# Q's memory slots by a selection product, its other columns by crossbar DMA, and scores on four column groups straight from the key ring

## The chip, the cores and the metric

The kernel runs on one core of one Trainium2 chip. The metric is the device time of one execution, in microseconds (us). "Before" and "after" are always the two kernels. Quoted times are medians. Ratios are computed from the mean time of one kernel's fast runs over the mean of the other's fast runs of the same rounds, so they are not quite the ratios of the medians.

## The reference, cut to what matters

```python
# x: (1, 2048, 640) bf16; 32 heads of 128; M = 8 memory slots; segments of 32 tokens
mem = mem0
for s in range(64):
    h = concat([mem, layernorm(x)[segment s]])           # 8 + 32 rows
    q, k, v = h @ Wq, h @ Wk, h @ Wv                     # 32 heads
    p = softmax(where(mask, q @ k.T * Dh**-0.5, -1e9))   # 40 x 40 for each head
    o = (p @ v) @ Wo
    mem = o[:8]                                          # the next segment needs this
    outs.append(o[8:])
h = x + concat(outs)
out = h + ((relu(g) * u) @ W_down)                       # g, u: gate and up products of layernorm(h)
```

Only the 8 memory rows tie one segment to the next. This makes a serial loop of 64 rounds; the feed-forward part at the end is one large block of matrix products.

## The kernel before

In each segment (a round of the loop) TensorE (PE) projects 32 columns: the 8 memory slots, and up to 24 "riders", tokens of later segments that fill the tile. Keys and queries of tokens are parked in a ring (`Kr`, `Qr`) until their segment comes. A projection leaves its result token by token; scores need it with the head dimension on the partitions, so it has to be transposed.

K goes through the crossbar (the DMA's transposing path, `DMA_TRANSPOSE` in the traces) into `KS`; Q goes through TensorE (`trans8`):

```python
project(a, ks, 1, (0, 1), BQ, spare=40)              # K of 32 columns
to_tok(BQ[0], 0, "act"); to_tok(BQ[1], 1, "dve")
dma_t(KS[...], tokp[0][:, :], ...)                   # crossbar, on the SP queue
loads()
...
project(a, ks, 0, (0, 1), (P0, P1), spare=40)        # Q
if s == NSEG - 2:
    load_gate_up()                                   # weights of the feed-forward part
...
project(a, ks, 2, (0, 1), (P2, P3), (0, 1), spare=16)    # a first piece of V
trans8(tok[2], ("tok", 2), tok[3], ("tok", 3), T0)       # eight 128x128 transposes
copy_op("dve", Qr[:, :, q, 0:M], slots(T0, 0, M), ...)   # Qm: the memory slots of Q
kx_mem(KS[:, :, 0:M], ("KS",))                           # KX: memory slots of K; waits for KS
if nr:
    evac_q(T0, t0, nr, M, "act")                         # riders of Q into the ring
    evac_k(KS, ("KS",), t0, nr, M, "dve")                # riders of K into the ring
# ... cut: a store and a load of the normalization rows ...
project(a, ks, 2, (0, 1), (P2, P3), (2, 3, 4), spare=24) # the rest of V
# ... cut ...
scores(s)                                                # reads KX and Qr
```

The program issues each engine's instructions in the order in which they are written, and in the traces below they run in that order. So the place of a copy in this list is its place in the queue of VectorE (DVE). In the same way all transfers that are written without another engine go to one queue, SP's, in order.

The scores are products with 64-column and 40-column tiles of `KX`, a copy that puts memory slots and tokens of two heads side by side:

```python
for k in range(8):
    for e in range(2):
        for cg in range(2):
            h = 4 * k + 2 * cg + e
            n = 64 - (SEG - M) * e
            i = pe.matmul(bank(...)[64 * cg:64 * cg + n, ...], KX[:, h, 0:n], Qr[:, h, q, :], ...)
```

Finally, the kernel fixes where the output product (the "Wo pass") falls within lines of 256 instructions of PE's stream. It does this with four marks, one for each s%4, and fills up with repeated weight loads in the projections (`spare`):

```python
PE_FIRST, PE_LINE = 64, 256
MARKS = (130, 108, 130, 130)
...
wo_pass(T1, MARKS[s % 4] if s > 3 else None)
...
G.align(PE_FIRST, PE_LINE)
```

The softmax here doesn't subtract the row's maximum and nothing guards it: scores larger than these inputs give would overflow.

## Time and profile before

| | before |
|---|---|
| Time, median of 3 runs (range) | 1146.69 us (1143.68 to 1147.58) |
| Span of the profiled execution | 1142.5 us |
| PE busy | 1083.2 us, 95% |
| PE idle just before the scores | 8.7 us |
| Period of a segment, mean over segments 4 to 60 | 14.00 us |
| First score, after the start of that segment's K projection | 7.42 us |
| DVE's first copy out of `KS`, on the same clock | 6.91 us |

X stands for the start of a segment's K projection throughout.

These lines are from the page of the kernel before: its span, the busy time of each engine, and the chain of work that ended last.

```profile
span 1142.5 us, 55213 instructions
...
PE 1083.2 (95%) x26294; PEld 573.2 (50%) x24948; DVE 614.2 (54%) x1603; ACT 357.4 (31%) x729; POOL 279.7 (24%) x567
...
PE 84%; DMA 7%; DVE 4%; SPq 3%; issue 1%; ACT 0%; DVEq 0%
PE ps L409 30%; PE ps L387 14%; PE ps L621 14%; PE ps L987 10%; DMA KS<-tok 4%; PE ps L429 3%; PE ps L549 3%; PE ps L635 3%; PE ps L1020 3%; SPq L355 3%; DMA Wo<-in_A_Wo_dram 3%; PE ps L586 2%; DVE TBf L525 1%; DVE act_r L526 1%; PE ps L659 1%
```

Read: TensorE is the limit nearly everywhere. The transfer of `KS` makes up 4% of the chain.

The second view is one line of the groups of the kernel before: line, engine, operation, names, shapes, count, then busy time and mean ns of one, then idle time before it and who ended it.

```profile
L549 PE MATMUL ps<-Qr,KX 128*64 128x40 bf16 (+1 forms) x2048 | 40.7, 184 | 8.7 <-DVE KX L438 8.5
```

In the 64 segments PE waits 8.7 us in all for what the scores need. One wait, in the last segment, is 4.5 us of that.

The third view is the timeline of segment 33 of the kernel before (X = 510.99): start, duration, instruction, and in brackets the idle time before it with its releaser. First DVE, then PE.

```profile
515.53 0.69 DVE L438 CAST tok<-ps 128x512 bf16<-128x512 f32 x1 [1.47 <-PE ps L387]
516.94 0.29 DVE L438 COPY Qr<-ps 128x256 bf16<-128x256 bf16 x1 [0.72 <-PE ps L429]
517.79 0.23 DVE L438 COPY KX<-KS 128x256 bf16<-128x256 bf16 x1 [0.56 <-DMA KS<-tok]
517.93 0.42 DVE L438 COPY Kr<-KS 128x256 bf16<-128x256 bf16 x2
```

```profile
516.28 0.62 PE L429 MATMUL ps<-ident,tok 128*128 128x128 bf16 x8
516.85 1.48 PE L409 MATMUL ps<-W,act_r 128*32 128x512 bf16 x24
518.26 0.63 PE L549 MATMUL ps<-Qr,KX 128*64 128x40 bf16 x32
```

The Qm copy fills a gap in which DVE would wait for `KS` anyway. The copy out of `KS` that the scores need (`KX`) is the first thing after the landing. The rider copies (`Kr`) come behind it. PE goes from V straight into the scores.

### The profile page before, as it was taken

What the parts mean: (1) busy time and instruction counts of PE and PEld (TensorE: products, weight loads), DVE (VectorE), ACT (ScalarE), POOL (GpSimd) and SP (SyncE); (2) the same over time, 40 slices, a digit from 0 to 9 for tenths busy, and PEclk for the clock granted to TensorE, in tenths of its full rate; (3) what the DMA queues carried; (4) which work ended last, traced back from release to release, by engine and by line L of the source; (5) the groups of instructions that cost most, each with busy time, mean ns of one, the idle gap of its engine ahead of it and who ended that gap; (6) DMA issues with size and microseconds to landing.
All of it is one profiled execution on the core that took longest, in us unless ns stands there. A gap on an engine that the chain in (4) does not pass through costs nothing.

```text
span 1142.5 us, 55213 instructions
## 1 busy us (share of the span) xinstructions
PE 1083.2 (95%) x26294; PEld 573.2 (50%) x24948; DVE 614.2 (54%) x1603; ACT 357.4 (31%) x729; POOL 279.7 (24%) x567
## 2 busy tenths in 40 slices
PE   5589999999999999999999999999999978999998
PEld 2345555555555555555455555555555545443443
DVE  3245656565656565656565666565656542553522
ACT  2113333333333333333333333333333312221220
POOL 1013333333323242414141414141414130000000
PEclk9989999999999999999999999999999998999999
DMA  9934454445444454545655455444545395132100
GB/s 354 377 75 78 65 72 65 72 66 75 65 75 66 72 73 65 78 92 80 87 74 92 78 93 72 73 74 63 74 60 71 58 229 166 35 81 71 29 18 24
DMA packets 214103, 102.45 MB, mean 90 GB/s; under 512 B 188032, under 2 KB 203456, under 8 KB 213872
## 3 DMA queue, kind: packets, MB, share of 16 engines
q1 hardware_dynamic: 196016, 82.96, 38.4%
q0 software_dynamic: 17664, 15.94, 7.3%
q8 instruction: 201, 3.29, 1.3%
q14 instruction: 30, 0.25, 0.1%
q10 hardware_dynamic: 192, 0.01, 0.0%
HBM read 36.79 MB, written 7.21 MB: 39 GB/s over the span
## 4 chain that ended last, share of the span: by engine, by line
PE 84%; DMA 7%; DVE 4%; SPq 3%; issue 1%; ACT 0%; DVEq 0%
PE ps L409 30%; PE ps L387 14%; PE ps L621 14%; PE ps L987 10%; DMA KS<-tok 4%; PE ps L429 3%; PE ps L549 3%; PE ps L635 3%; PE ps L1020 3%; SPq L355 3%; DMA Wo<-in_A_Wo_dram 3%; PE ps L586 2%; DVE TBf L525 1%; DVE act_r L526 1%; PE ps L659 1%
## 5 line engine op out<-in xcount | busy, mean ns | idle before, releaser
L409 PE MATMUL ps<-W,act_r 128*32 128x512 bf16 x6209 | 436.6, 383 | 15.5 <-DVE act_r L526 4.3
L355 POOL DMA_DIRECT2D Vr<-Vp x376 | 188.2, 508 | 564.8 <-ACT Vp L436 381.2
L409 PEld LDWEIGHTS ps<-W,act_r 128*32 128x32 bf16 x6209 | 168.7, 97 | 199.8 <-issue 104.6
L436 ACT ACTIVATE tok<-ps 128x512 bf16<-128x512 f32 x191 | 110.6, 595 | 268.6 <-PE ps L387 209.6
L621 PE MATMUL ps<-Wo,oT 128*32 128x160 bf16 x8320 | 161.1, 237 | 10.9 <-DMA Wo<-in_A_Wo_dram 8.8
L387 PE MATMUL ps<-W,act_r 128*32 128x512 bf16 x1671 | 168.2, 379 | 0.0
L621 PEld LDWEIGHTS ps<-Wo,oT 128*32 128x32 bf16 x8320 | 147.2, 99 | 40.6 <-DVE oT L438 29.3
L438 DVE CAST tok<-ps 128x512 bf16<-128x512 f32 x131 | 90.6, 692 | 128.5 <-PE ps L387 68.2
L436 ACT ACTIVATE Qr<-ps 128x768 bf16<-128x768 bf16 (+3 forms) x110 | 69.2, 658 | 86.7 <-DVE Qr L438 79.4
L409 PE MATMUL ps<-W,act_e 128*32 128x512 bf16 x900 | 89.2, 381 | 0.0
L387 PE MATMUL ps<-W,act_e 128*32 128x512 bf16 x900 | 88.8, 379 | 0.0
L674 DVE TENSOR_TENSOR ox<-ps,rx 128x512 bf16<-128x512 f32 x128 | 82.5, 686 | 2.2
L355 POOL DMA_DIRECT2D attn_d<-wtok x64 | 46.9, 732 | 113.6 <-ACT wtok L436 113.6
L525 DVE STREAM_TRANSPOSE TBf<-ps 128x160 f32<-128x160 f32 x64 | 22.4, 351 | 94.5 <-PE ps L621 94.5
L1002 DVE TENSOR_TENSOR hT<-g,ps 128x512 bf16<-128x512 bf16 (+1 forms) x56 | 38.4, 688 | 54.5 <-PE ps L987 50.3
L406 PEld LDWEIGHTS <-act_r 128*32 128x32 bf16 x1433 | 42.8, 96 | 48.9 <-issue 13.5
L987 PE MATMUL ps<-xn2T,Wg 128*128 128x512 bf16 x260 | 65.2, 382 | 0.0
L987 PE MATMUL ps<-xn2T,Wu 128*128 128x512 bf16 x260 | 64.6, 379 | 0.0
L1020 PE MATMUL ps<-Wd,hT 128*128 128x320 bf16 (+1 forms) x240 | 63.3, 300 | 0.0
L1000 ACT ACTIVATE g<-ps 128x512 bf16<-128x512 f32 (+1 forms) x56 | 32.4, 593 | 93.8 <-PE ps L987 93.8
L387 PE MATMUL ps<-Wd,hT 128*128 128x320 bf16 x208 | 56.9, 299 | 0.0
L429 PE MATMUL ps<-ident,tok 128*128 128x128 bf16 x664 | 50.9, 220 | 5.2 <-DVE tok L438 3.3
(92 smaller groups left out, 1127.4 us busy)
## 6 DMA issues: line engine op xcount, KB each, us to landing
Vr<-Vp POOLq DMA_DIRECT2D x124, 48.8 KB, 1.9
W<-in_A_Wk_dram SPq DMA_DIRECT2D x2, 2560.0 KB, 12.9
W<-in_A_Wq_dram SPq DMA_DIRECT2D x2, 2560.0 KB, 25.2
W<-in_A_Wv_dram SPq DMA_DIRECT2D x2, 2560.0 KB, 27.2
Wo<-in_A_Wo_dram SPq DMA_DIRECT2D x2, 2560.0 KB, 28.5
xt<-in_A_x_dram SPq DMA_DIRECT2D x30, 160.0 KB, 3.0
Vr<-Vp POOLq DMA_DIRECT2D x128, 32.5 KB, 2.3
attn_d<-wtok POOLq DMA_DIRECT2D x64, 40.0 KB, 3.8
```

What stands on the lines that cost most here:

```text
L355: add(eng, lambda e: e.dma_start(dst, src), r=r, w=w, dma=True)
L387: return pe.add_instruction(mybir.InstMatmult(name=nc.get_next_instruction_name(), engine=mybir.EngineType.PE, ins=[pe.lower_ap(rhs), pe.l ...
L406: pe.ldweights(act[:, c, :], tile_position=(0, 32 * g))
L409: ins = pe.matmul(*a, start=(c == 0), stop=(c == DC - 1), skip_group_check=True)
L429: ins = pe.matmul(bank_bf(b)[:, k * 128:(k + 1) * 128], t[:, (k % 4) * 128:(k % 4 + 1) * 128], ident[:, :], is_transpose=True)
L436: add("act", lambda a: a.activation(dst, src, ACTF.Copy), r=r, w=w)
L438: add("dve", lambda v: v.tensor_copy(dst, src), r=r, w=w)
L621: i = pe.matmul(bank(bk)[32 * gg:32 * gg + 32, 0:160], oT[:, hb, :], w[:, gg], start=(hb == ORDER[0]), stop=(hb == ORDER[31]), skip_group_ ...
L674: add("dve", lambda v, kh=kh: v.tensor_tensor(ox[:, :, kh, :], src[:, :, kh, 0:128], ap(rx, kh, [[2, 4], [0, 128]]), ALU.mult), r=[B(b0 + ...
L987: ins = pe.matmul(bank(bk), w[:, c, lo:lo + 128], xn2T[par][:, c, :], start=(c == 0), stop=(c == DC - 1))
L1002: add("dve", lambda v: v.tensor_tensor(hT[par][lo:128, j, :], g1[gi][lo:128, :], bank(bu)[lo:128, :], ALU.mult), r=[B(bu), ("g1", gi)], w= ...
L1020: i = pe.matmul(*a, start=(j == 0), stop=(j == FC - 1), skip_group_check=True)
```

## The change

The intent is to take work off TensorE and VectorE:

1. Only the 8 memory slots of Q are needed at once. TensorE gets them with a selection product: eight products with 32 moving columns of the identity in place of eight 128-column transposes (`pick_mem`). The riders of Q go through the crossbar into `QS`, as K does.
2. The extra query tokens of every fourth segment (`fin`) go through the crossbar too.
3. The scores run on four column groups of 32, with memory slots straight from `KS` and tokens straight from the ring `Kr`. `KX` and its two copies in each segment go.
4. Orders move: `evac_k` comes ahead of the Qm copy, since the scores now need the ring; loads wait for `KS`; the normalization of later rows moves behind the attention; half of the transposes of `om` become full-width; marks are chosen anew.

The core of the diff, with cuts marked by "...":

```diff
-    MARKS = (130, 108, 130, 130)
+    MARKS = (150, 98, 114, 130)
...
+    def pick_mem(bk):
+        def f(pe):
+            for k in range(8):
+                ins = pe.matmul(bank(bk)[:, 32 * k:32 * k + 32], tok[2 + k // 4][:, (k % 4) * 128:(k % 4 + 1) * 128],
+                                ap(ident, 0, [[32, 4], [1, M]]), start=True, stop=True, skip_group_check=True)
+            return ins
...
+    def trans_q():
+        dma_t(QS[:].rearrange(...), tokp[1][:, :], [("tok", 2), ("tok", 3)], [("QS",)])
...
             for k in range(8):
-                for e in range(2):
-                    for cg in range(2):
-                        h = 4 * k + 2 * cg + e
-                        n = 64 - (SEG - M) * e
-                        i = pe.matmul(bank((P0, P1)[e])[64 * cg:64 * cg + n, 40 * k:40 * k + 40], KX[:, h, 0:n],
+                for a in range(2):
+                    for g in range(4):
+                        h = 4 * k + g
+                        p, lh = (32 * (g ^ 1), Kr[q][:, h, :]) if a == 0 else (32 * g, KS[:, h, 0:M])
+                        i = pe.matmul(bank((P0, P1)[g % 2])[p:p + (M if a else 32), 40 * k:40 * k + 40], lh,
                                       Qr[:, h, q, :], start=True, stop=True, skip_group_check=True)
...
         def fin():
-            trans8(tok[2], ("tok", 2), tok[3], ("tok", 3), T0)
-            evac_q(T0, t0, 32, 0, "act")
+            trans_q()
+            late.append(lambda: evac_q(QS, ("QS",), t0, 32, 0, "act"))
...
-                dma(xt[:, :], x_ap[128 * e2:128 * e2 + 128, :], w=[("xt",)])
+                dma(xt[:, :], x_ap[128 * e2:128 * e2 + 128, :], r=[("KS",)], w=[("xt",)])
...
                 to_tok(P0, 2, "act")
                 to_tok(P1, 3, "dve")
+                if nr:
+                    trans_q()
...
             if not last:
-                trans8(tok[2], ("tok", 2), tok[3], ("tok", 3), T0)
-                copy_op("dve", Qr[:, :, q, 0:M], slots(T0, 0, M), [B(T0)], [("Qm", q)])
-            kx_mem(KS[:, :, 0:M], ("KS",))
+                pick_mem(T0)
             if nr:
-                evac_q(T0, t0, nr, M, "act")
                 evac_k(KS, ("KS",), t0, nr, M, "dve")
+            if not last:
+                copy_op("dve", Qr[:, :, q, 0:M], bank(T0)[:, 0:256].rearrange("p (h t) -> p h t", t=M), [B(T0)], [("Qm", q)])
...
+                evac_q(QS, ("QS",), t0, nr, M, "act")        # behind exp_x
...
-        trans_om()
+        trans_om(128 if s % 4 < 2 else 32)
...
-        kx_x(seg_slot(s + 1))
```

More of the change, by code (lines that the diff above doesn't have):

```diff
@@ L271, in build_kernel @@
     tok = [tokp[i // 2][:, 512 * (i % 2):512 * (i % 2) + 512] for i in range(4)]
-    KX = ar.alloc("KX", [128, H, 2 * SEG], BF16)
     KS = ar.alloc("KS", [128, H, SEG], BF16)
     Kr = [ar.alloc(f"Kr{i}", [128, H, SEG], BF16) for i in range(RING // SEG)]
+    QS = ar.alloc("QS", [128, H, SEG], BF16)
     Qr = ar.alloc("Qr", [128, H, RING // SEG, M + SEG], BF16)
@@ L337, in build_kernel @@
         add("dve", lambda v, g=g: v.memset(mbd[32 * g:32 * g + M, 1, 8 * g:8 * g + 8], BIG), r=[("mbd",)], w=[("mbd",)])
-    add("dve", lambda v: v.memset(KX[:], 0.0), w=[("KX", "m"), ("KX", "x")])
+    for b in (P0, P1):
+        add("dve", lambda v, b=b: v.memset(bank(b), 0.0), w=[B(b)])
     add("dve", lambda v: v.memset(oT[:], 0.0), w=[("oT", "m"), ("oT", "x")])
@@ L432, in trans8 @@
         add("pe", f, r=[k0, k1, ("ident",)], w=[B(b)])
+    def pick_mem(bk):
[4 more added lines that the diff above has]
+            return ins
+        add("pe", f, r=[("tok", 2), ("tok", 3), ("ident",)], w=[B(bk)])
+    def trans_q():
+        dma_t(QS[:].rearrange("p h t -> p (h t)").rearrange("p (k r) -> p k r", r=128), tokp[1][:, :],
+              [("tok", 2), ("tok", 3)], [("QS",)])
     def copy_op(eng, dst, src, r, w):
@@ L455, in evac_k, with evac_q @@
             copy_op(eng, Kr[q][:, :, o:o + m], src[:, :, lo:lo + m], [skey], [("Kr", q)])
-    def evac_q(b, t0, n, lo, eng):
+    def evac_q(src, skey, t0, n, lo, eng):
         for q, o, m, lo in pieces(t0, n, lo):
-            copy_op(eng, Qr[:, :, q, M + o:M + o + m], slots(b, lo, lo + m), [B(b)], [("Qr", q)])
+            copy_op(eng, Qr[:, :, q, M + o:M + o + m], src[:, :, lo:lo + m], [skey], [("Qr", q)])
     def seg_slot(s):
@@ L529, in build_kernel @@
     oTe_keys = [("oTe", q) for q in range(4)]
-    def kx_mem(src, skey):
-        copy_op("dve", ap(KX, 0, [[4 * SEG, 16], [3 * SEG, 2], [1, M]]), src.rearrange("p (k e) t -> p k e t", e=2), [skey],
-                [("KX", "m")])
-    def kx_x(q):
-        copy_op("dve", ap(KX, SEG, [[4 * SEG, 16], [1, 2 * SEG]]), ap(Kr[q], 0, [[2 * SEG, 16], [1, 2 * SEG]]), [("Kr", q)],
-                [("KX", "x")])
     def scores(s):
@@ L544, in f @@
             for k in range(8):
-                for e in range(2):
-                    for cg in range(2):
-                        h = 4 * k + 2 * cg + e
-                        n = 64 - (SEG - M) * e
-                        i = pe.matmul(bank((P0, P1)[e])[64 * cg:64 * cg + n, 40 * k:40 * k + 40], KX[:, h, 0:n],
+                for a in range(2):
[3 more added lines that the diff above has]
+                        i = pe.matmul(bank((P0, P1)[g % 2])[p:p + (M if a else 32), 40 * k:40 * k + 40], lh,
                                       Qr[:, h, q, :], start=True, stop=True, skip_group_check=True)
             return i
-        add("pe", f, r=[("KX", "m"), ("KX", "x"), ("Qm", q), ("Qr", q)], w=[B(P0), B(P1)])
+        add("pe", f, r=[("KS",), ("Kr", q), ("Qm", q), ("Qr", q)], w=[B(P0), B(P1)])
     def s_view(lo, hi):
@@ L595, in norm_om, with trans_om @@
             r=[B(T1), ("rm",)], w=[("om",)])
-    def trans_om():
+    def trans_om(tile):
         def f(pe):
             for a in range(2):
-                for c in range(4):
-                    i = pe.matmul(bank_bf(T1)[32 * c:32 * c + 32, a * 128:(a + 1) * 128], om[:, a, 32 * c:32 * c + 32],
+                for c in range(0, 128, tile):
+                    i = pe.matmul(bank_bf(T1)[c:c + tile, a * 128:(a + 1) * 128], om[:, a, c:c + tile],
                                   ident[:, :], is_transpose=True)
@@ L761, in opening_back @@
             else:
-                evac_q(bk, 32 * (n - 1), 32, 0, eng)
+                evac_q(slots(bk, 0, SEG), B(bk), 32 * (n - 1), 32, 0, eng)
             return
@@ L765, in opening_back @@
         if j == 1:
-            kx_mem(slots(bk, 0, M), B(bk))
+            copy_op("dve", KS[:, :, 0:M], slots(bk, 0, M), [B(bk)], [("KS",)])
             evac_k(slots(bk, 0, SEG), B(bk), 64, RID, M, "act")
@@ L769, in opening_back @@
             copy_op("dve", Qr[:, :, q, 0:M], slots(bk, 0, M), [B(bk)], [("Qm", q)])
-            evac_q(bk, 64, RID, M, "act")
+            evac_q(slots(bk, 0, SEG), B(bk), 64, RID, M, "act")
     for j in (1, 0):
@@ L785, in build_kernel @@
         opening_back(j, 2, P2)
-    kx_x(seg_slot(0))
     scores(0)
@@ L874, in loads @@
                 ln1_load(nb, xt, ("xt",))
+            if s % 4 == 1 and s - 2 in EARLY:
+                e = EARLY.index(s - 2)
+                dma(xn2_d[:, :, 128 * e:128 * e + 128], chunks_of(at[:, :]), r=[("at",)], w=[("xn2_d", e)])
+                if ln:
+                    ln1_load(nb, xt, ("xt",))
         if s == 0:
@@ L884, in build_kernel @@
                   [("tok", 0), ("tok", 1)], [("KS",)])
-            loads()
             for f in late:
@@ L888, in build_kernel @@
             late = []
+            loads()
             if not last:
@@ L894, in build_kernel @@
                 to_tok(P1, 3, "dve")
-            n = n_rows(nb) if s % 4 == 2 and ln else 128 if e2b is not None else 0
-            if n:
-                row_scale(xt, ("xt",), n, xt, ("xt",))
-                dma_t(chunks_of(at[:, :])[:, :, 0:n], xt[0:n, :], [("xt",)], [("at",)])
+                if nr:
+                    trans_q()
             project(a, ks, 2, (0, 1), (P2, P3), (0, 1), spare=16)
             if not last:
-                trans8(tok[2], ("tok", 2), tok[3], ("tok", 3), T0)
-                copy_op("dve", Qr[:, :, q, 0:M], slots(T0, 0, M), [B(T0)], [("Qm", q)])
-            kx_mem(KS[:, :, 0:M], ("KS",))
+                pick_mem(T0)
             if nr:
-                evac_q(T0, t0, nr, M, "act")
                 evac_k(KS, ("KS",), t0, nr, M, "dve")
-            if e2b is not None:
-                dma(xn2_d[:, :, 128 * e2b:128 * e2b + 128], chunks_of(at[:, :]), r=[("at",)], w=[("xn2_d", e2b)])
-                if ln:
-                    ln1_load(nb, xt, ("xt",))
+            if not last:
+                copy_op("dve", Qr[:, :, q, 0:M], bank(T0)[:, 0:256].rearrange("p (h t) -> p h t", t=M), [B(T0)], [("Qm", q)])
             project(a, ks, 2, (0, 1), (P2, P3), (2, 3, 4), spare=24)
@@ L926, in build_kernel @@
                 v_riders(t0, nr)
-            if s % 4 == 2 and ln:
-                ln1_back(nb, chunks_of(at[:, :]), [("at",)], "pool")
+                evac_q(QS, ("QS",), t0, nr, M, "act")
         units, evac, nfin = extra_units(s)
@@ L942, in build_kernel @@
         filler(3)
-        trans_om()
+        trans_om(128 if s % 4 < 2 else 32)
         mask_x()
+        n = n_rows(nb) if s % 4 == 2 and ln else 128 if e2b is not None else 0
+        if n:
+            row_scale(xt, ("xt",), n, xt, ("xt",))
         filler(4)
@@ L957, in build_kernel @@
         pv_x(s, P0)
+        if n:
+            dma_t(chunks_of(at[:, :])[:, :, 0:n], xt[0:n, :], [("xt",)], [("at",)])
+            if s % 4 == 2:
+                late.append(lambda nb=nb: ln1_back(nb, chunks_of(at[:, :]), [("at",)], "pool"))
         if nfin:
```

## The prediction

> **What bounds it now.** The engine table has PE busy 95%; the chain that ended last is 84% PE, 7% DMA, 4% DVE. In the timeline of a plain segment (start X = 510.99 us, period 13.70) PE runs: K and Q projections, a V piece, 8 transposes of Q (X+5.29, 56 ns apart, next projection at +0.57), the rest of V, scores (X+7.27; 0.56 long), fillers, pv, Wo pass 2.40. The groups table puts 8.7 us of PE idle before scores, 5.2 before the transposes. Every fourth segment (s%4 = 3) has 8 more transposes for extra Q tokens (0.55 on the chain); such periods are 14.05. A second chain is nearly as long: K evacuated (X+3.1), crossbar transpose lands in 3.1 to 3.7 us, DVE starts the KX copy at about X+6.75, waiting for the landing 49 times of 63 (waits view). Scores start 0.28 to 1.1 us after that copy starts, mean 0.55: about 0.25 us of slack.
>
> **On PE.** (a) Pick: 32 moving columns, not 128. 56 ns apart becomes about 25: the Trainium skill ("TensorE: Matmul & The Clock Gate", the passage on the 56 ns gap) gives a floor of about 25 ns start to start; here the 40-column scores step 28 ns per round. Saves 0.2 x 62 = 13. (b) Scores in 128x32 tiles as the projections: no mode change ("TensorEngine Tiling (Array Packing)", Key Properties: that drains). Gap to the first score 309 ns against 216 between projection rounds; that and the exit, 109, shrink together by about 0.17. 16 rounds as before, of four matmuls, not two: estimated 28 to 35 ns each against 28. Saves 6 to 12. (c) Extra-Q transposes go: 15 x 0.4 = 6. (d) trans_om as two full matmuls in half the segments: two mode changes, +0.1 x 31 = +3.
>
> **Moved.** KX copies (0.42 and 0.22) leave DVE; 77 crossbar transposes (about 1.3 us of issue each) join the SP queue behind KS; I expect KS landing little changed. row_scale leaves the path before scores, the x load waits for KS: that should end single stalls (1.4 us before scores at 546.8, 0.7 at 504.5), about 3 us.
>
> **What gives gain back.** DVE's new order: wait for KS, evac_k (about 0.3), Qm copy from fp32 PSUM (about 0.42, as the 128x256 om product), then scores. Before, scores followed the landing by 0.28; now by about 0.75. PE would be ready at about X+6.95, DVE lets it go at X+7.5: a new stall of about 0.5 us. Over the 62 measured slacks, scores start on average 0.2 us later in place of 0.3 earlier, which eats (a) and most of (b).
>
> **Sum.** +15 (later start of scores, (a) included) -9 (b) -6 (c) +3 (d) -3 (stalls) is about 0; without the DVE-order stall about -28. Weighing the two: 1138 us, range 1118 to 1156. Faster by over 2%: 0.20; within 2%: 0.76; slower: 0.04.
>
> **What would show it.** Right: PE busy down about 25 us; picks about 25 ns apart; score rounds 28 to 35 ns; PE idle before scores up from 8.7 to 20-35 us, released by DVE's Qr copy; all periods about alike. Wrong: idle before scores under 10 us (KS lands earlier; then 1118 or less); picks still 56 ns apart (weight-load bound); score rounds of 50 ns or more; KS landing past 4 us because Q transposes crowd it (then slower); Wo passes longer than 2.16 us from first to last start.

## The result, and the profile after

| | before | after |
|---|---|---|
| Time, median of 4 runs each (range) | 1145.97 us (1143.68 to 1147.58) | 1187.82 us (1187.11 to 1189.63) |
| Ratio of the fast runs | | 1.0369, interval 1.0347 to 1.0392 |
| Span of the profiled execution, granted clock | 1142.5 us, 0.990 | 1187.9 us, 0.981 |
| PE busy | 1083.2 us | 1073.4 us |
| PE idle just before the scores | 8.7 us | 50.2 us |
| Period of a segment | 14.00 us | 14.63 us |
| First copy out of `KS`, after X | 6.91 us | 7.16 us |
| First score, after X | 7.42 us | 8.08 us |
| `KS`, issue to that first copy | 3.63 us | 3.89 us |

The change made the kernel 3.7% slower. The extra 45.4 us of span divide into 2.5 us up to the score of segment 5, 35.3 us from there to the score of segment 61 and 7.3 us from the score of segment 62 to the end; the rest is rounding and the one segment between. Between 130 and 900 us the mean granted clock is 1.00 in both traces, so the loop did not grow by a lower clock. The 2.5 us at the start are within what other runs scatter there (127.7 to 131.4 us up to that score), so they are not read further.

From the page of the kernel after:

```profile
span 1187.9 us, 55568 instructions
...
PE 1073.4 (90%) x28030; PEld 501.2 (42%) x23537; DVE 584.2 (49%) x1477; ACT 349.2 (29%) x729; POOL 280.4 (24%) x567
...
PE 61%; DMA 24%; DVE 7%; SPq 3%; issue 3%; ACT 1%; DVEq 0%
DMA KS<-tok 17%; PE ps L388 13%; PE ps L410 13%; PE ps L627 12%; PE ps L995 10%; DMA QS<-tok 4%; PE ps L555 3%; PE ps L641 3%; PE ps L1028 3%; SPq L356 3%; DMA Wo<-in_A_Wo_dram 2%; PE ps L592 2%; DVE Qr L452 2%; DVE tok L452 2%; DVE TBf L539 2%
```

PE and DVE both do less, as intended. But the chain now runs through the transfer of `KS` for 17% of the span, where it was 4%.

The scores in the groups of the kernel after:

```profile
L555 PE MATMUL ps<-Qr,Kr 128*32 128x40 bf16 x2048 | 40.9, 187 | 50.2 <-DVE Qr L452 45.1 <-DMA KS<-tok 5.0
```

Nearly all idle time ends on one instruction, DVE's copy into `Qr`, the Qm copy. The timeline of segment 34 of the kernel after (X = 544.96) shows why, first DVE and then PE:

```profile
549.55 0.69 DVE L452 CAST tok<-ps 128x512 bf16<-128x512 f32 x1 [0.43 <-PE ps L388]
552.28 0.43 DVE L452 COPY Kr<-KS 128x512 bf16<-128x512 bf16 x2 [2.04 <-DMA KS<-tok]
552.63 0.42 DVE L452 CAST Qr<-ps 128x256 bf16<-128x256 f32 x1
```

```profile
550.32 0.36 PE L439 MATMUL ps<-ident,tok 128*128 128x32 bf16 x8
...
551.70 0.39 PE L388 MATMUL ps<-W,act_r 128*32 128x512 bf16 x4
553.10 0.20 PE L555 MATMUL ps<-Qr,Kr 128*32 128x40 bf16 x4 [1.01 <-DVE Qr L452]
```

The selection product is done at 550.68. The Qm copy could run then, and DVE is idle for 2.04 us. But the copy stands behind `evac_k` in the queue, and that waits for `KS` until 552.28. So two copies follow the landing before the scores, where one did before. PE stands for 1.01 us.

### The profile page after: what moved, and what is told of

Read it like the earlier page. It is cut to its first block, busy times and chain, and to the rows that moved or that the text cites. A ratio compares the mean times of both kernels' runs of the same rounds, so it can differ in the third digit from the quotient of the medians.

```text
span 1187.9 us, 55568 instructions
## 1 busy us (share of the span) xinstructions
PE 1073.4 (90%) x28030; PEld 501.2 (42%) x23537; DVE 584.2 (49%) x1477; ACT 349.2 (29%) x729; POOL 280.4 (24%) x567
## 4 chain that ended last, share of the span: by engine, by line
PE 61%; DMA 24%; DVE 7%; SPq 3%; issue 3%; ACT 1%; DVEq 0%
DMA KS<-tok 17%; PE ps L388 13%; PE ps L410 13%; PE ps L627 12%; PE ps L995 10%; DMA QS<-tok 4%; PE ps L555 3%; PE ps L641 3%; PE ps L1028 3%; SPq L356 3%; DMA Wo<-in_A_Wo_dram 2%; PE ps L592 2%; DVE Qr L452 2%; DVE tok L452 2%; DVE TBf L539 2%
## 5 line engine op out<-in xcount | busy, mean ns | idle before, releaser
L410 PE MATMUL ps<-W,act_r 128*32 128x512 bf16 x4383 | 403.1, 387 | 16.8 <-DMA W<-in_A_Wv_dram 3.0
L388 PE MATMUL ps<-W,act_r 128*32 128x512 bf16 x3497 | 346.8, 381 | 0.2 <-issue 0.2
L410 PEld LDWEIGHTS ps<-W,act_r 128*32 128x32 bf16 x4383 | 121.9, 98 | 273.7 <-issue 208.3
L410 PE MATMUL ps<-W,act_e 128*32 128x512 bf16 x900 | 91.2, 385 | 0.0
L388 PE MATMUL ps<-W,act_e 128*32 128x512 bf16 x900 | 90.8, 382 | 0.0
L555 PE MATMUL ps<-Qr,Kr 128*32 128x40 bf16 x2048 | 40.9, 187 | 50.2 <-DVE Qr L452 45.1
L450 ACT ACTIVATE Qr<-QS 128x512 bf16<-128x512 bf16 (+3 forms) x108 | 71.2, 693 | 38.3 <-DMA QS<-tok 38.3
L565 ACT ACTIVATE om<-ps 128x128 bf16<-128x128 f32 x63 | 17.5, 278 | 211.8 <-PE ps L555 211.8
L452 DVE COPY Kr<-KS 128x256 bf16<-128x256 bf16 (+2 forms) x93 | 24.7, 293 | 109.3 <-DMA KS<-tok 109.3
L555 PEld LDWEIGHTS ps<-Qr,Kr 128*32 128x32 bf16 x2048 | 34.9, 94 | 92.2 <-DVE Qr L452 83.9
## 6 DMA issues: line engine op xcount, KB each, us to landing
W<-in_A_Wk_dram SPq DMA_DIRECT2D x2, 2560.0 KB, 12.7
```

Source lines behind the costliest of these rows:

```text
L388: return pe.add_instruction(mybir.InstMatmult(name=nc.get_next_instruction_name(), engine=mybir.EngineType.PE, ins=[pe.lower_ap(rhs), pe.l ...
L410: ins = pe.matmul(*a, start=(c == 0), stop=(c == DC - 1), skip_group_check=True)
L450: add("act", lambda a: a.activation(dst, src, ACTF.Copy), r=r, w=w)
L452: add("dve", lambda v: v.tensor_copy(dst, src), r=r, w=w)
L555: i = pe.matmul(bank((P0, P1)[g % 2])[p:p + (M if a else 32), 40 * k:40 * k + 40], lh, Qr[:, h, q, :], start=True, stop=True, skip_group_c ...
```

## The experiments

Fourteen kernels gave sixteen results: `e13` repeats `e9`, and `e16` repeats `e10`. Ratios are to the kernel before, in the same rounds. "First copy" and "first score" are means over segments 4 to 60 of the time after X in the profiled execution. "Loop" is the time from the score of segment 5 to that of segment 61, "end" the time from the score of segment 62 to the end.

| run | what | median us | ratio (95% interval) | first copy | first score | loop | end |
|---|---|---|---|---|---|---|---|
| before | | 1145.97 | 1 | 6.91 | 7.42 | 784.2 | 216.2 |
| after | | 1187.82 | 1.0369 (1.0347 to 1.0392) | 7.16 | 8.08 | 819.5 | 223.5 |
| e1_qm_first | after, Qm copy ahead of evac_k | 1160.38 | 1.0162 (1.0122 to 1.0201) | 7.10 | 7.37 | 789.3 | 225.2 |
| e2_q_pe | after, all of Q by TensorE | 1156.86 | 1.0135 (1.0105 to 1.0164) | 6.86 | 7.60 | 796.0 | 218.7 |
| e3_ring_only | e2 with Qm first | 1145.24 | 1.0026 (0.9999 to 1.0053) | 6.85 | 7.28 | 781.3 | 219.0 |
| e4_qm_queue | e1, queue orders mended | 1155.67 | 1.0115 (1.0078 to 1.0152) | 7.06 | 7.27 | 786.4 | 223.0 |
| e5_late_evac | e3, evac_k behind mask_x | 1144.30 | 1.0016 (0.9992 to 1.0039) | | 7.26 | 778.2 | 221.1 |
| e6_qs_after_ks | e1, QS waits for KS | 1193.98 | 1.0443 (1.0402 to 1.0484) | 7.58 | 7.81 | 826.3 | 224.6 |
| e7_full | e4, evac_k behind mask_x | 1148.90 | 1.0060 (1.0027 to 1.0092) | | 7.37 | 784.1 | 223.8 |
| e8_pick_only | before, with pick and QS for riders | 1143.59 | 1.0008 (0.9984 to 1.0032) | 6.83 | 7.25 | 776.4 | 222.9 |
| e9_marks_after | after, marks moved by 45 | 1180.89 (fast runs) | 1.0304 (1.0281 to 1.0327) | | | | |
| e10_mended | e8, two orders mended | 1137.42 | 0.9912 (0.9895 to 0.9929) | 6.97 | 7.35 | 775.6 | 218.7 |
| e11_marks_before | before, marks moved by 45 | 1166.29 | 1.0168 (1.0149 to 1.0186) | 6.63 | 7.54 | 802.6 | 220.4 |
| e12_mended_marks | e10, marks moved by 45 | 1152.15 | 1.0046 (1.0027 to 1.0064) | 6.66 | 7.30 | 788.6 | 219.7 |
| e13_marks_after_again | e9 again | 1188.22 | 1.0347 (1.0316 to 1.0379) | 6.82 | 7.75 | 817.8 | 222.6 |
| e14_before_qm_last | before, Qm copy last | 1158.48 | 1.0107 (1.0069 to 1.0144) | 6.86 | 7.68 | 794.9 | 217.0 |
| e15_before_late_evac | before, evac_k behind mask_x | 1142.00 | 0.9961 (0.9940 to 0.9981) | 6.90 | 7.44 | 780.8 | 216.8 |
| e16_mended_again | e10 again | 1137.37 | 0.9943 (0.9916 to 0.9971) | 6.90 | 7.28 | 771.6 | 219.8 |

In `e5` and `e7` the first copy out of `KS` no longer comes at the landing, so it is left out. The trace of `e9` is explained below.

The theory: the loss is the order of two copies on DVE (ORDER). Rivals: the crossbar and the SP queue are crowded by the new transposes, so that `KS` or Q comes late (QUEUE, CROWDING); the new scores are slow on PE.

### The order of two copies: e1, e2, e3 and e14

`e1_qm_first` swaps the two copies in the kernel after, and nothing else:

```diff
-            if nr:
-                evac_k(KS, ("KS",), t0, nr, M, "dve")
             if not last:
                 copy_op("dve", Qr[:, :, q, 0:M], bank(T0)[:, 0:256]..., [("Qm", q)])
+            if nr:
+                evac_k(KS, ("KS",), t0, nr, M, "dve")
```

> The changed kernel with one swap: DVE's copy of Q's memory columns (Qm) is issued before the copy of K riders (evac_k), which waits for the KS crossbar transpose. Theory ORDER (the Qm copy sits behind the KS landing, so scores start some 0.8 us after it): the first score moves from 8.08 us after the K projection's start to about 7.3, PE idle before scores falls from 50 us to under 25, time 1188 to about 1145-1155. Theory CROWDING (the 77 added Q transposes make KS land later, 7.16 instead of 6.91 after the projection's start, and this is what costs): landing stays at 7.1-7.2 and time stays at 1170 or more.

Measured: 1160.38 us. By the ratios, each of its own rounds, that is 24 us less than the kernel after (1.0162 against 1.0369); by the medians, which come from different rounds, it is 27. The first score moved from 7.16 + 0.92 to 7.10 + 0.27 us. The line of the groups of `e1_qm_first`:

```profile
L555 PE MATMUL ps<-Qr,Kr 128*32 128x40 bf16 x2048 | 41.2, 186 | 13.7 <-DMA KS<-tok 12.9
```

The idle time fell from 50.2 to 13.7 us, and none of it is put down to DVE any more. So the order of two copies costs some 24 us in this kernel. It is not all: `e1` is still 1.6% slower than before.

`e2_q_pe` takes the Q transposes back to TensorE, riders and extra tokens alike, and keeps the scores from the ring and DVE's new order. (The full-width transpose of `om` is then used in three segments of four.) `e3_ring_only` is `e2` with the same swap as in `e1`.

```diff
         def fin():
-            trans_q()
-            late.append(lambda: evac_q(QS, ("QS",), t0, 32, 0, "act"))
+            trans8(tok[2], ("tok", 2), tok[3], ("tok", 3), T0)
+            evac_q(slots(T0, 0, SEG), B(T0), t0, 32, 0, "act")
...
-                if nr:
-                    trans_q()
...
-                pick_mem(T0)
+                trans8(tok[2], ("tok", 2), tok[3], ("tok", 3), T0)
...
-                copy_op("dve", Qr[:, :, q, 0:M], bank(T0)[:, 0:256]..., [("Qm", q)])
+                copy_op("dve", Qr[:, :, q, 0:M], slots(T0, 0, M), [B(T0)], [("Qm", q)])
+            if nr:
+                evac_q(slots(T0, 0, SEG), B(T0), t0, nr, M, "act")
...
-                evac_q(QS, ("QS",), t0, nr, M, "act")
-        trans_om(128 if s % 4 < 2 else 32)
+        trans_om(128 if s % 4 < 3 else 32)
```

> The changed kernel with all of Q transposed by TensorE again (8 transposes, Q's other columns copied from PSUM, no QS transposes at all, the extra-Q transposes back); scores from the key ring and the DVE order of the changed kernel are kept; trans_om takes the full form in three of four segments so that the instruction lines stay aligned. CROWDING: KS lands as early as in the kernel before (6.9) and the time comes back to 1147 or below. ORDER: KS lands at 6.9 but scores still start some 0.6 us after it, about 7.5; idle before scores stays at 15-25 us on DVE's Qr; time 1150-1162. QUEUES (Q's transposes stand in in-order queues: ACT's copy of extra Q before the Q evacuation, the last segment's behind the weight loads): the segments with s%4=0 no longer have 2 us waits and the tail is 7 us shorter; time about 1170 if this alone were the cause.

> As e2, with the Qm copy before evac_k: the scores part of the change alone, on the kernel before's way of transposing Q. ORDER: against e2 0.3 to 0.4 us per segment, 18-25 us; first score at about 7.2; time about 1130-1140, under the kernel before, as the KX copy after the landing and two mode changes are gone. If the ring scores themselves cost time, it stays above 1147.

Measured: 1156.86 and 1145.24 us. The swap is worth 11.6 us here. With it, the scores from the ring, together with the moved loads, the moved normalization and the full-width transposes that `e3` keeps, are level with the kernel before (1.0026). I had expected 1130 to 1140 us, a gain, and it did not come. PE's idle time before the scores in `e3` is 3.1 us. So the scores on four column groups are not the cause, and crowding by Q isn't needed for a loss of 1%, since `e2` has no transposes of Q on the crossbar.

`e14_before_qm_last` is the test from the other side: the suspected order alone, put into the kernel before.

```diff
             if not last:
                 trans8(tok[2], ("tok", 2), tok[3], ("tok", 3), T0)
-                copy_op("dve", Qr[:, :, q, 0:M], slots(T0, 0, M), [B(T0)], [("Qm", q)])
             kx_mem(KS[:, :, 0:M], ("KS",))
             if nr:
                 evac_q(T0, t0, nr, M, "act")
                 evac_k(KS, ("KS",), t0, nr, M, "dve")
+            if not last:
+                copy_op("dve", Qr[:, :, q, 0:M], slots(T0, 0, M), [B(T0)], [("Qm", q)])
```

> The kernel before with the Qm copy on VectorE moved behind the two copies that wait for KS (KX, then evac_k), nothing else. ORDER theory: from the first of those copies to the first score there are then 0.23 us (KX) + 0.42 us (evac_k, mean over the segments) + 0.29 us (Qm) + about 0.18 us of handshake = 1.1 us where it was 0.51: the first score comes about 0.6 us later in each of some 60 segments, 30 to 40 us in all: 1175 to 1187 us, ratio 1.026 to 1.036, and nearly all idle time of TensorE before the scores ends on DVE's Qr copy. Rival (TensorE would have been late anyway, or the copies overlap with something else): under 15 us.

Measured: 1158.48 us, 1.0107, some 12 us. The direction and the releaser are as the order theory says; the size is a third of what I expected, and it is under the 15 us that I gave the rival. The groups of `e14_before_qm_last`:

```profile
L549 PE MATMUL ps<-Qr,KX 128*64 128x40 bf16 (+1 forms) x2048 | 40.7, 184 | 22.7 <-DVE Qr L438 17.3 <-DVE KX L438 4.5
```

The timeline of DVE and PE in segment 40 of `e14_before_qm_last` shows the mistake in my sum:

```profile
627.20 0.22 DVE L438 COPY KX<-KS 128x256 bf16<-128x256 bf16 x1
627.34 0.35 DVE L438 COPY Kr<-KS 128x768 bf16<-128x768 bf16 x1
627.61 0.28 DVE L438 COPY Qr<-ps 128x256 bf16<-128x256 bf16 x1
...
627.94 0.63 PE L549 MATMUL ps<-Qr,KX 128*64 128x40 bf16 x32
```

I added durations. But queued copies overlap: they start 0.14 and 0.27 us apart (also in the median of all segments), where they are listed with 0.22 and 0.35. From the first copy to the first score it took 0.74 us here and 0.82 in the mean, not 1.1. And PE is ready at about X + 7.27 at the earliest in this kernel, so that a part of the delay was free. The order alone is worth 12 us in the kernel before and in `e3`; in the kernel after it is worth some 24, where `KS` lands later as well, and the Qm copy reads fp32 (0.42 us against 0.28). How the other 12 us divide between these two was not tried.

### One queue for everything: e4, e6 and e7

What is left in `e1` shows in two places. The first is the segments 31, 35, 39 and 43, in which rows of the feed-forward part are prepared, and whose loads now wait for `KS`. SP's queue and ScalarE (ACT) of the kernel after, around segments 31 and 32:

```profile
503.58 1.80 SPq L359 DMA_TRANSPOSE KS<-tok  x1
507.25 0.34 SPq L356 DMA_DIRECT2D xt<-in_A_x_dram  x1
507.64 0.42 SPq L356 DMA_DIRECT2D at<-attn_d  x1
508.17 7.44 SPq L359 DMA_TRANSPOSE QS<-tok  x2
```

```profile
512.51 0.84 ACT L450 ACTIVATE Qr<-QS 128x768 bf16<-128x768 bf16 x1 [2.49 <-DMA QS<-tok]
...
520.00 1.06 ACT L450 ACTIVATE Qr<-QS 128x1024 bf16<-128x1024 bf16 x1 [2.56 <-DMA QS<-tok]
...
521.38 0.58 ACT L450 ACTIVATE tok<-ps 128x512 bf16<-128x512 f32 x1
```

The load of `xt` waits for `KS` to land, at the head of the one queue. The transpose of Q stands behind it until 508.17. ACT then waits for `QS` twice, and its copy of the next Q projection (`tok`) stands behind the second wait. PE (the kernel after, the same segment) waits for that:

```profile
522.11 0.35 PE L439 MATMUL ps<-ident,tok 128*128 128x32 bf16 x8 [2.27 <-ACT tok L450]
```

There are five such waits in the kernel after, 9.9 us in all (four behind these segments, one in segment 60). The second place is the end. At segment 62 the weights of the feed-forward part are loaded. In the kernel before the queue holds K's transpose, then the weights; Q does not use it. In the kernel after Q's transpose is behind the weights:

```profile
964.88 4.95 SPq L356 DMA_DIRECT2D Wgu<-in_B_W_up_dram  x1
969.92 6.77 SPq L359 DMA_TRANSPOSE QS<-tok  x1
976.73 2.72 SPq L359 DMA_TRANSPOSE oT<-ox  x1
982.04 1.23 SPq L359 DMA_TRANSPOSE KS<-tok  x1
```

The issue of one transpose takes 6.77 us here (the median for `KS` is 1.86 in this kernel), and the next `KS` follows it. The end (score of segment 62 to the last instruction) grew from 216.2 to 223.5 us.

`e4_qm_queue` is `e1` with three moves: the late copy of the extra Q comes after Q's own copies on ACT, and the loads, those of the weights too, come after `trans_q` on SP.

```diff
-            late.append(lambda: evac_q(QS, ("QS",), t0, 32, 0, "act"))
+            late_q.append(lambda: evac_q(QS, ("QS",), t0, 32, 0, "act"))
...
-            loads()
...
-                if s == NSEG - 2:
-                    load_gate_up()
                 to_tok(P0, 2, "act")
                 to_tok(P1, 3, "dve")
+                for f in late_q:
+                    f()
+                late_q = []
                 if nr:
                     trans_q()
+                if s == NSEG - 2:
+                    load_gate_up()
+            loads()
```

> e1 plus three moves in the in-order queues: ACT's copy of the extra Q columns goes after the evacuation of Q (before: ahead of it), the x load that waits for KS goes behind the Q transpose on SP, the weight loads of the last segments go behind the Q transpose. QUEUES: the 2.3 us waits for pick in the segments after s=31, 35, 39, 43 go, and the tail after the last score is 216 us instead of 223; 12-18 us less than e1, time about 1130-1140. ORDER alone or CROWDING alone: within 5 us of e1.

Measured: 1155.67 us against 1160.38, on the same chip. PE's waits for ACT's `tok` are gone from the top of its waits, but there is a new one: 7.4 us for DVE's `Pbd`, six times. The loop got 2.9 us shorter, the end 2.2. This misses the expectation: 12 to 18 us less were expected and 4.7 came, inside the 5 us that stood for the rivals; the intervals of the two ratios overlap, and the end stayed at 223.0 us, not 216. So the waits show the queue here, and the time hardly does.

`e6_qs_after_ks` asks about crowding. It is `e1` with Q's transposes made to wait until `KS` has landed, so that they can't share the crossbar with it:

```diff
-              [("tok", 2), ("tok", 3)], [("QS",)])
+              [("tok", 2), ("tok", 3), ("KS",)], [("QS",)])
```

> e1 with the Q transpose made to wait for the KS landing. Same work, same bytes, only apart in time. CROWDING: from issue to landing of KS falls from 3.87 us to about 3.6 as in the kernel before and in e2, e3 (3.53-3.63); idle before scores, 13.7 us in e1, falls under 8; the time falls by 5 to 12 us. If the Q transposes do not disturb KS: landing stays at 3.8 or more, the time stays or rises by the later evacuation of Q's columns on ACT.

Measured: 1193.98 us, 1.0443 where `e1` had 1.0162: some 32 us more. This is the clearest case of the queue: a wait that was put on one transfer holds everything behind it, the next `KS` too, whose issue comes 3.94 us after X instead of 3.23 (`e1`). On crowding it says less. The mean from issue to first copy fell from 3.87 us to 3.64, as CROWDING had expected (its gain in time did not come). But most of that fall is where the issue itself came later: with s%4 = 0 it moved from 3.18 to 4.93 us after X, and the landing from 4.07 to 3.28. Where the issue stayed within 0.1 us, `KS` took 4.08 us (`e1` 3.92, before 3.71) with s%4 = 1 and 3.48 (`e1` 3.57) with s%4 = 2. So in the segments in which `KS` is latest, keeping Q's transposes away does not bring it sooner; for the mean, `e6` decides nothing.

`e7_full` is the whole change with the orders mended: `e4` with `evac_k` moved behind `mask_x`, where DVE has time, and the loads moved only where it matters.

```diff
-            if nr:
-                evac_k(KS, ("KS",), t0, nr, M, "dve")
...
         trans_om(128 if s % 4 < 2 else 32)
         mask_x()
+        if s > 0 and nr:
+            evac_k(KS, ("KS",), t0, nr, M, "dve")
```

> e4 with evac_k after mask_x as in e5 and with the loads moved behind the Q transpose only in the segments where they wait for KS (e4 had moved them in all, and its s%4=1 segments lost some 0.4 us between scores and pv). All known order faults of the change mended, the Q crossbar transposes kept. Expected: 10 to 20 us under e4: about 1136-1146. If it stays over 1150, something else in the change costs that I have not named.

Measured: 1148.90 us, 1.0060. All parts of the change are in it, and of the 42 us that the change cost 7 are left. I had expected 10 to 20 us less than `e4`; by the ratios it is 6. In the trace, which is of the slowest of the four runs (1154.52 us), the excess is in the end (223.8 us against 216.2) and 2.5 us before the score of segment 5; the loop is level: PE's waits there name 8.3 us of "issue" in the last Wo passes and 5.0 us for `KS`. I did not settle what the issue time is; the weights fill the DMA engines at that moment (a busy share of 1.0), and the records have the instruction packets among the DMA's. Part of the recovery is no part of the change: the moved `evac_k` gains 0.4% in the kernel before as well (`e15`, below).

`e5_late_evac` moves `evac_k` in the same way in `e3`.

> e3 (ring scores, Q on TensorE, Qm first) with evac_k moved on DVE from ahead of scores to after mask_x, since its rows are needed only by later segments. Finding to test: in e3 scores start 0.14 us earlier than in the kernel before, but the Wo pass only 0.02, because the softmax chain after scores (exp, Pbd on DVE, pv) took it back: from pv to the transposes of om 1.35-1.50 us against 1.21-1.35 before, DVE running evac_k in between. If so, that stretch falls back to about 1.25-1.3 and the time falls 5-9 us under e3, to about 1134-1140. If DVE is not what holds that stretch (but TensorE's latency, or trans_om's form), the time stays within 2 us of e3.

Measured: 1144.30 us, 1.0016: no gain in time, where 5 to 9 us were expected. The loop gained 3.1 us over `e3`, and the end gave 2.1 back.

### Why KS lands later: e9, e11, e12 and e13

`KS` takes 0.25 us longer from issue to first use in the kernel after (0.6 in the segments with s%4 = 1). For s%4 = 1, `e6` speaks against Q's transposes. In the packet records something else stands out: queue 8, "instruction", fetches packets of 16,384 bytes, and such a packet took 0.9 to 1.9 us where the median packet of queue 1, which carries the transposes, took 0.018. The table sorts segments 4 to 60 of four kernels (before, after, `e11`, `e13`) by the start of such a packet relative to the issue of `KS`:

| start of the packet, us from the issue of KS | segments | KS, issue to first copy, mean us |
|---|---|---|
| more than 1.4 earlier | 101 | 3.16 |
| 1.4 to 1.0 earlier | 14 | 3.39 |
| 1.0 to 0.6 earlier | 35 | 3.67 |
| 0.6 to 0.2 earlier | 43 | 3.88 |
| 0.2 earlier to 0.3 later | 18 | 4.08 |
| more than 0.3 later | 12 | 4.07 |
| none within 2.2 earlier and 1.5 later | 5 | 3.20 |

The kernel before has 15 of its 57 segments in the first row, the kernel after 8. With the means of the table, the counts of the two kernels alone give 3.62 and 3.80 us: 0.17 of the 0.26 us between them. The rest is not accounted for: in the fourth and fifth rows `KS` is later in the kernel after (3.99 and 4.22 us) than before (3.82 and 3.72, the last from three segments). In the first row the transposes of Q make no difference: 3.21 and 3.12 us in the kernel after and `e13`, 3.13 and 3.18 in the kernel before and `e11`. But `e2` and `e3`, without transposes of Q, took 3.53 and 3.58 us, less than the table's means give for their counts (3.60 and 3.69), so a share of Q's transposes in the rest is not excluded. All this is a correlation. The alignment marks allow an experiment: moving all four by 45 leaves the filling from segment 5 on as it is (the counts of weight loads differ in segments 2 to 4 alone), and moves the places at which a line of 256 instructions ends by 45 instructions.

```diff
-    MARKS = (150, 98, 114, 130)     # after:  e9, e13
+    MARKS = (105, 53, 69, 85)
-    MARKS = (130, 108, 130, 130)    # before: e11 (and e12, in e10)
+    MARKS = (85, 63, 85, 85)
```

> The kernel after, with nothing changed but the places of four alignment marks of the instruction stream, each 45 instructions earlier. It tests what makes KS land late. FETCH theory: a 16 KB packet of the instruction queue, which in the kernel after begins 2.6 to 2.9 us after the K projection begins, holds up the crossbar transpose of the attention output, and KS behind it. Moved to about 1.6 to 2.0 us it is over before that transpose has data: issue to landing of KS falls from 3.89 us to about 3.4 in the mean, and in the segments with s%4=1 from 4.32 to 3.2 to 3.6; the first score comes 0.3 to 0.4 us earlier, so 15 to 25 us less than the kernel after, ratio to the kernel before about 1.015 to 1.025. CROWDING theory (the four transposes of Q share the crossbar with KS and make it late): landing stays at 3.8 to 3.9, time at 1183 to 1190. In both, PE's idle time before the scores still ends on DVE's Qr copy.

> The kernel before, with nothing changed but the places of its four alignment marks (earlier by about 45). FETCH theory: issue to landing of KS falls from 3.63 to about 3.3 us; the scores of the kernel before are bound by TensorE within 0.15 us by then, so the gain is at most 5 to 9 us: 1134 to 1140 us. If the fetch falls in the output pass instead, that pass lengthens beyond 2.17 us and the time stays or grows. CROWDING theory: landing stays 3.6, time unchanged.

> The run e10 with the alignment marks 45 instructions earlier. FETCH theory: KS lands 0.3 us sooner and, since this form has less TensorE work ahead of the scores, more of it is gained than in e11: 1122 to 1132 us. CROWDING theory: as e10.

> The same kernel as e9, for a profile in the fast state. FETCH theory: the instruction packet begins before 2.1 us after the start of the K projection, and issue to landing of KS is 3.1 to 3.5 us in the mean (3.89 in the kernel after); the time of e9 (1180, only 8 us less than after) is then explained as in e11: the moved fetches starve projections, whose matmul busy time (605 us over the two W lines in the kernel before) grows by 10 to 40 us. CROWDING theory: landing 3.8 or more.

Measured: the landing moved as the fetch theory says, in all three. Issue to first copy: 3.63 to 3.19 us (`e11` against before), 3.63 to 3.23 (`e12` against `e10`), 3.89 to 3.33 (`e13` against after). No transpose was moved, so the place of the fetch is enough to move the landing by this much. `e11` has 51 of 57 segments in the first row of the table.

The gain did not follow. `e11` became 1.7% slower, where I had expected 5 to 9 us less; `e12` lost what `e10` had gained (1152.15 us, expected 1122 to 1132); `e9` and `e13` stayed within 0.7% of the kernel after (1.0304 and 1.0347, where 1.015 to 1.025 was expected). The top of PE's waits in `e11_marks_before` (waiter, releaser, then total us, times, longest):

```profile
PE ps L659 <- issue: 17.0, 16, 1.5
PE ps L621 <- DMA Wo<-in_A_Wo_dram: 6.9, 2, 6.4
PE ps L376 <- DVE xt L370: 6.7, 1, 6.7
```

and in `e13_marks_after_again`:

```profile
PE ps L665 <- issue: 19.5, 17, 1.6
PE ps L555 <- DVE Qr L452: 12.7, 23, 1.0
```

The wait for the Qm copy went from 45.1 to 12.7 us in `e13`, but a new wait appeared: 19.5 us in the product behind the Wo pass (L659 of the kernel before, L665 of the kernel after). Nearly all of these waits, 0.4 to 1.6 us each, are in the segments with s%4 = 1: fifteen of them in either kernel. PE waits there for nothing that the profile shows. Since only the places of the line ends were moved, the likely cause is that the next line has not arrived when PE gets there; that is an inference, no record shows PE waiting for a line. The period of those segments went from 13.86 to 15.30 us in `e11`. The projections take longer as well: in `e11` the transposes of Q start 5.56 us after X instead of 5.36, so that the first score comes later (7.54 against 7.42) although `KS` is there sooner. So the old marks were the better compromise: a fetch that holds up `KS` a little rather than PE.

The profiled execution of `e9` ran at a granted clock of 0.18 and took 5431.92 us; its other five runs are between 1179 and 1187. Its trace says nothing about the kernel, which is why `e13` repeats it, and the run is left out of the median in the table (with it the median is 1182.87).

### What is left of the change's gain: e8, e10, e15 and e16

`e8_pick_only` puts into the kernel before only what needs no new order: the selection product, and the riders' Q through the crossbar. It keeps `KX` and transposes the extra tokens on TensorE. As the expectation says, there was no room for `QS` beside `KX`, so `QS` borrows the tile `ox`.

```diff
+    QS = ox[:].rearrange(...)
+    def pick_mem(bk): ...                # as in the change
+    def trans_q(): ...                   # into ox
...
+                if nr:
+                    trans_q()
...
-                trans8(tok[2], ("tok", 2), tok[3], ("tok", 3), T0)
-                copy_op("dve", Qr[:, :, q, 0:M], slots(T0, 0, M), [B(T0)], [("Qm", q)])
+                pick_mem(T0)
+                copy_op("dve", Qr[:, :, q, 0:M], bank(T0)[:, 0:256]..., [B(T0)], [("Qm", q)])
```

> The kernel before with the other half of the change alone: TensorE picks only the memory columns of Q, the other columns by crossbar DMA in every segment (into the ox tile, as there is no room beside KX; the extra Q tokens stay on TensorE), KX scores and DVE order as before. The pick saves TensorE 0.2 us per segment, but scores wait for KX, which waits for KS. ORDER plus a KS bound: first score at 7.3-7.5, no gain: time within 6 us of the kernel before, slightly slower if CROWDING holds (KS landing 3.8 or later: up to 12 us slower). If TensorE's work were the bound: 1130-1135.

Measured: 1143.59 us, 1.0008. The loop is 7.8 us shorter than before and the end 6.7 us longer, so nothing is left. `e10_mended` therefore moves the load of the weights behind Q's transpose, and `evac_k` behind `mask_x`:

```diff
-                if s == NSEG - 2:
-                    load_gate_up()
                 to_tok(P0, 2, "act")
                 to_tok(P1, 3, "dve")
                 if nr:
                     trans_q()
+                if s == NSEG - 2:
+                    load_gate_up()
...
             if nr:
-                evac_k(KS, ("KS",), t0, nr, M, "dve")
...
         mask_x()
+        if s > 0 and nr:
+            evac_k(KS, ("KS",), t0, nr, M, "dve")
```

> The kernel before with only the selection product and the scores from the key ring: every transpose of Q stays on TensorE as in the run e8, evac_k moved behind mask_x, and the load of the gate and up weights issued behind the Q transpose of its segment. It asks whether the parts of the change that held gain over the kernel before when its queue costs are left out. QUEUE theory: the 6 to 8 us that e5 and e8 gained in the loop were given back at the end by the order of transfers on one queue; with the load behind, the tail (score of segment 62 to the end) is 216 to 219 us and the loop 774 to 778: 1133 to 1138 us, ratio 0.991 to 0.997. LATENCY theory (the end of the kernel pays for anything that arrives sooner, whatever the queue does): tail 222 or more, time within 0.2% of before.

The recorded text misnames the kernel: the edit has no scores from the ring but keeps `KX`, and it sends the riders' Q through the crossbar, as `e8` does. Its numbers are judged here for the kernel that was run.

Measured: 1137.42 us, 0.9912. The end came down from 222.9 to 218.7 us and the loop stayed at 775.6, as expected. This version is faster than both kernels, by 0.6 to 0.9% against the kernel before (`e16`, `e10`). Whose merit is it? `e15_before_late_evac` makes the move of `evac_k` in the kernel before alone, and `e16_mended_again` repeats `e10` on the same chip.

> The kernel before with evac_k moved behind mask_x on VectorE, nothing else. If the gain of e10 in the loop (8.6 us between the scores of segments 5 and 61: scores 0.07 us sooner, the stretch from the value product to the transpose of om 0.09 us shorter) is that of the order alone: 1136 to 1142 us, ratio 0.990 to 0.996, that stretch 0.09 us shorter and the first score where it was. If it is that of the change's parts: ratio 0.998 to 1.002.

> The same kernel as e10, on the chip of e15: ratio to before 0.989 to 0.994, as there.

Measured: 1142.00 us (0.9961) and 1137.37 us (0.9943, at the edge of what was expected). The stretch from the value product to the transpose of `om` is shorter in both by the same amount, for instance 1.18 against 1.24 us in the segments with s%4 = 3. In `e15` the first score is where it was (7.44), in `e16` it comes at 7.28. The intervals of the two ratios overlap. So about 0.4% belongs to one moved copy, which has nothing to do with the change; what the selection product and the crossbar for riders add to it is 0.2% by these ratios, and isn't separated from nothing by the timing alone. In another round `e10` was further ahead (0.9912), without a run of `e15` beside it.

## Why the prediction was wrong

I predicted 1138 us (1118 to 1156) and gave "slower by over 2%" a chance of 0.04. It took 1187.82 us. Taken point by point:

**What bounds it: right.** The second chain (K, crossbar, DVE) was said to have about 0.25 us of slack. The time went where that slack was: the chain of the kernel after runs through `KS<-tok` for 17%.

**(a) the selection product: right.** The eight products start 25 ns apart (median; the eight transposes 56), as the Trainium skill, "TensorE: Matmul & The Clock Gate", in "Wait — 56ns, not 53.3ns?", has for products of 32 columns. The next projection starts 0.295 us after the first of them instead of 0.565: 0.27 us less, where I said 0.2. All of it went into waiting: PE was to be busy 25 us less and is busy 9.8 us less.

**(b) the scores: right on the parts, wrong on the worth.** The gap to the first score fell from 309 to 206 ns where nothing else held it (in three segments of the kernel after, and in most of `e3`), which agrees with the Trainium skill, "TensorEngine Tiling (Array Packing)", "Key Properties", that a change of tiling mode drains. The rounds take 32 ns, at 0.485 us for fifteen, as estimated, against 30 before (0.453 us). But from the first score to the Wo pass it takes 3.45 us, 0.06 more than before (3.39). I had 9 us of gain less 3 for (d); it is a loss of 3.5 us over 56 periods. In the segments with full-width transposes of `om` (s%4 = 0 and 1) the stretch grew from 3.39 to 3.52 us, about what (d) was to cost; in the others it stayed at 3.39. So (b) gained nothing by the Wo pass.

**(c) the extra Q: right in its place, but it was paid for elsewhere.** The time from the Wo pass to the next segment fell by 0.35 us in the segments with s%4 = 3 (3.46 to 3.11), 5 us in all. The next segment waits for the late copy, as shown above: there the selection product comes at 5.98 us after X in place of 5.44.

**"I expect KS landing little changed": wrong.** It takes 0.25 us more in the mean and 0.6 where s%4 = 1. I had named a late landing as a risk, through crowding by Q's transposes; the landing is late, and what could be shown to move it is another thing, the place of an instruction fetch (`e11`, `e12`, `e13`), which accounts for 0.17 us of the mean by the table; the rest stays open.

**"That should end single stalls, about 3 us": wrong.** It made new ones: 9.9 us of waits for `tok`, and 7.3 us at the end. The Trainium skill, "DMA: Bandwidth & Descriptors", "Issuing engines are not separate DMA queues", says that transfers started by the scalar, sync or gpsimd engine run on the same 16 DMA engines and interleave; it does not speak of instruction packets, and here moving those of queue 8 (0.9 to 1.9 us) moved the landing of a transpose of queue 1. Besides, the queue that issues the transposes is one, and a transfer that waits for `KS` holds those behind it. I counted the 77 new transposes as 1.3 us of issue each and did not ask what stands in front of each.

**What gives gain back: the mechanism right, the size of its step about right, and then not given full weight.** I predicted 0.75 us from the landing to the first score, released by DVE's Qr copy. It is 0.77 to 0.82 us in three of the four kinds of segments (1.24 in the fourth, where the selection product is late). Idle time before the scores was to be 20 to 35 us; it is 50.2.

The step that failed is the sum, "+15 (later start of scores, (a) included)": scores were to start 0.2 us later and start 0.65 us later, 37 us over 56 periods, because the landing moved by 0.25 us, because every fourth segment waits for its selection product (0.11 us in the mean), and because the step from landing to score was 0.51 us before, not the 0.55 that I took, and 0.77 to 0.82 after. The other terms made up no gain: (b) came with the other sign, and the stalls that were to end grew. Then there is "weighing the two: 1138": an average of "about 0" and "about -28" that gives the second some 30%. The second had no ground, since the order of the two copies stands in the diff and the landing in the trace; whether DVE stalls was not open.

| term, us | predicted | measured |
|---|---|---|
| later start of the scores | +15 | +37 (0.65 x 56) |
| from scores to the Wo pass: (b) with (d) | -6 | +3.5 (0.06 x 56) |
| from the Wo pass to the next segment: (c) | -6 | -4.6 (0.08 x 56) |
| single stalls, end | -3 | +7.3 at the end, +2.5 at the start; stalls within segments are in the first row |
| sum | about 0 | 45.7, against 45.4 us of span |

**Shown and not shown.** That the order of the two copies costs some 24 of the 42 us is shown by undoing it (`e1`) and, at 12 us, by doing it alone (`e14`). That the orders on SP and ACT with the move of `evac_k` make up most of the rest is shown by `e7` (1.0060) as a whole; `e4`, the queue orders alone, was not separated from `e1` by its time. And since the move of `evac_k` gives 0.4% without the change (`e15`, 0.9961), the change with its orders mended is still about 1% slower than the kernel before with the same move. That the place of the instruction fetch moves the landing is shown by moving it; that it is the whole reason for the later landing is not. That PE's new waits in `e11` and `e13` are waits for instructions is inferred. What starves the last Wo passes in `e7` is open.

## What to carry to other kernels

Before moving work off the busiest engine, find the second chain and its slack, and write down for each engine and each queue what stands in front of each instruction in the new order: a copy whose data is ready loses its time behind one that waits, and so does a transfer. Take the delay of queued copies from their start times, not from the sum of their durations. If the trace has timed both what a thing waits for and its place in the queue, count the stall in full and don't average it with a wish.

## What the Trainium skill lacked or had wrong

- "Runtime: NRT & Kernel Launch", "Instruction fetch mechanics", says that instructions come in blocks of 16 KiB by a DMA queue and that crossing a boundary is mostly hidden. The blocks agree (packets of 16,384 bytes). What it lacks: such a packet took 0.9 to 1.9 us, and `KS`, a crossbar transpose, needed 3.16 us when it began early enough and 3.9 to 4.1 us when it began close to the issue. Moving line ends by 45 instructions changed the landing by 0.4 to 0.56 us and the time by up to 1.7%.
- "DMA: Bandwidth & Descriptors", "Issuing engines are not separate DMA queues": it has the shared engines, but this section does not say what a wait in front of one transfer does to the next ones issued from the same engine. One added wait (`e6`) delayed the issue of the next `KS` by 0.70 us in the mean (against `e1`) and cost some 32 us.
